# Delta-rule attention and a top-1 mixture of experts: weight splits moved between steps, slot counts kept in PSUM, the last result block in halves

## The chip, the cores and the metric

The kernel runs on one core of a Trainium2 chip. The metric is the device time of one execution in microseconds, as a median of several runs.

## What is computed

The reference has two stages. The first is an attention with a delta rule: each of 4 x 8 heads carries a state of 48 x 48 that each token reads and then updates. The second sends each of the 3,072 rows of x (384 wide) to the one of eight experts that has its largest logit.

```python
for t in range(S):                       # S = 768, D = 48
    kt, vt, bt = (k_n[:, :, t], v[:, :, t], beta[:, :, t, None])
    y[:, :, t] = np.einsum('bhd,bhde->bhe', q[:, :, t], state)
    v_old = np.einsum('bhde,bhd->bhe', state, kt)
    state = state + bt[:, :, :, None] * np.einsum('bhd,bhe->bhde', kt, vt - v_old)
...
logits = x @ w_gate                      # x: 3072 x 384, 8 experts
expert_idx = np.argmax(logits, axis=1)
...
for e in range(E):
    h = np.maximum(x[expert_idx == e] @ w1[e], 0.0)      # 384 -> 1024
    out[expert_idx == e] = gate_w[expert_idx == e, None] * (h @ w2[e])
```

## The kernel before

**Steps.** The 3,072 tokens are 24 blocks of 128, n = 0 to 23, four batch entries by six stretches of time. A block needs the state that the block four before it left. Each is solved in four sub-blocks of 32 rows, and the sub-blocks of four different blocks run in one step, so that the steps t = 0 to 26 form a skewed pipeline: block n begins in step n and ends in step n + 3. Lines 967 to 1016 issue a step, in this order: mask, residual(t) (TensorE L446 and L458, then VectorE's L465, which subtracts it from v), the x rows of the block that has just ended (TensorE L543 into a bank `xp`, ScalarE L544 copying the row out), apply(t) (TensorE L473, four copies of ScalarE L478 to `u`), and finish(t-3) in four parts: L493, the small products L279 with ScalarE's copy L291 (`pm`), the state products L503 into a bank `sb` with ScalarE's copies L507 (`st`, which the residual of the next step reads), and L513 with L517 (`yt`, which the next x rows read).

**Places.** Between these parts stand seven calls beside(t, 0) to beside(t, 6), the places 0 to 6 of a step. There the other work is issued: loads that are due (list `off`), the inverses of the blocks to come (VectorE), the slot groups (up to FINE[i] parts of a generator a place), weight splits where the table WSL names (t, i), and pieces of expert 0's early work where ES does. The order in which an engine takes instructions is the order of issue, so these tables set each queue by hand.

**Slots.** When a group of blocks has ended (four blocks up to n = 11, two up to 19, one from 20 on; W4 = 12, W1 = 4), emit_slots (L547) finds each row's expert and its place in the expert's list. VectorE makes the one-hot matrix `ohb` in five operations (L562 to L579). TensorE counts into columns of the bank `xp` that hold no x rows: `ohb` by a triangle of ones (L584) and by ones (L587), each group anew. VectorE adds a running `base` (L593), moves it on (L594), masks the positions (L607) and reduces them to slots (L620). POOL then scatters the rows by indirect DMA (L628) to a table in DRAM. The row buffers come from pool `rp`, tag "row", with two buffers (L524 to L526). After block 17 (EU = 18) expert 0's first two blocks of tokens can be read: load_main(0, 0, 2) at L636. The last two blocks (DEF = 2) do not go through DRAM; for them VectorE makes a selection matrix `one` (L616), and TensorE multiplies the rows by it (L848).

**Weight splits.** Products of expert weights run on pairs of high and low parts. split (L665) is a ScalarE cast (L666) and a VectorE subtraction (L667) from a raw buffer; SP then loads the next raw piece into a ring of three. Eight of these stand in the loop, by WSL.

**The tail.** Expert 0 is started early on its first two blocks of tokens, in the order of the string EO: x (transposes L806), h (a block of the first layer), y (a result block, 24 matmuls L792), and t and o, which are parts of rest() (L835): the third block's transposes, then the last 64 columns, from the late rows (L848) and from a part read from DRAM (L850). The places of these in the loop are ES, and after the loop EF. dummy(8) and dummy(3) in rest() are filler matmuls without a use of their own (L660). After the tail the pool `lp` is closed and the experts 0 to 7 run one after the other; L782 is their first layer.

Of the kernel before, what the change touches and what calls it, by code (L numbers as in the profile page):

```python
# [8 lines left out]
F32 = mybir.dt.float32  # L9
# [33 lines left out]
def deltanet_moe(ctx, tc, qT, kT, kr, v, beta, w_gate, w1, w2, out):  # L43
# [27 lines left out]
    def constants():  # L71
        nc.gpsimd.memset(esel, 0.0)
        for p in range(NP):
# [8 lines left out]
        nc.gpsimd.memset(ones, 1.0)  # L82
        iota(last_i, [[1, CAP - 128 * NG]], 128 * NG)
# [28 lines left out]
    W1 = 4  # L112
# [6 lines left out]
    EU = 18  # L119
    TS = 5  # L120
# [15 lines left out]
    sb_ = [pss.tile([128, 512], F32, name=f"sb{j}")[:, 0:2 * NP * D].rearrange("p (b n d) -> p b n d", b=2, n=NP)  # L136
           for j in range(2)]
# [344 lines left out]
    def finish(n):  # L482
# [16 lines left out]
        if not last:  # L499
            sb = sb_[b // 2][:, b % 2]  # L500
            for h in range(H):
                r = slice(64 * (h % 2), 64 * (h % 2) + D)
                nc.tensor.matmul(sb[r, h // 2, :], lhsT=tiles[tb][b]["kn"][:, h], rhs=u[:, h, :],  # L503
                                 start=(tb == 0 and b % 2 == 0 and h < 2), stop=True, skip_group_check=True)
# [41 lines left out]

    def emit_slots(tb, b, w, parts, rl):  # L547
# [3 lines left out]
        def small(nm, shape, dt=F32):  # L551
            return lp.tile(shape, dt, name=f"{nm}{tb}_{b}", tag=f"{nm}{w}", bufs=1 if w > 1 else 2)
# [36 lines left out]
        dst = xg if tb * B + b < NN - DEF else xt  # L589
# [3 lines left out]
        V.tensor_tensor(out=pos, in0=both(base), in1=pp[:, 0:w, :], op=ALU.add)  # L593
        V.tensor_tensor(out=base, in0=base, in1=pp[:, w, :], op=ALU.add)  # L594
# [5 lines left out]
        if tb * B + b + w == NN - DEF:  # L600

            V.scalar_tensor_tensor(out=base, in0=lim, scalar=float(128 * NG - CAP), in1=base, op0=ALU.add, op1=ALU.max)
            nc.scalar.copy(out=late, in_=base)
        if tb * B + b + w == EU:
            V.scalar_tensor_tensor(out=base, in0=lim, scalar=float(128 * G0 - CAP), in1=base, op0=ALU.add, op1=ALU.max)

        noted(V.tensor_tensor(out=pos, in0=pos, in1=ohb, op=ALU.mult))  # L607
# [27 lines left out]
        if tb * B + b + w == EU:  # L635
            load_main(0, 0, G0)  # L636
        if tb * B + b + w == NN - DEF:
# [160 lines left out]
    def early():  # L798
# [36 lines left out]
    def rest():  # L835
# [450 lines left out]
```

## Time and profile before

| | us |
|---|---|
| median of 3 runs | 525.61 (523.99 to 525.97) |
| the profiled execution | 521.81 |
| its span | 519.70 |
| TensorE busy in the span | 482.6 (93%) |
| VectorE | 339.5 (65%) |
| ScalarE | 254.1 (49%) |
| POOL | 112.3 (22%) |

Times in the text are microseconds from the start of the span of the profiled execution, and names such as L473 are lines of the kernel before. A bracket behind a row of the timeline gives the time that the engine stood idle ahead of it and what ended that. A row gathers instructions of one kind that follow one another: x64 are 64 of them, and the time beside it is that of all.

### The profile page before, as it was taken

How to read it: one execution, taken by the hardware profiler on the slowest of the kernel's cores; microseconds unless marked ns; L12 is line 12 of the kernel's file. 1: busy time of each engine (PE TensorE's matmuls, PEld its weight loads, DVE VectorE, ACT ScalarE, POOL GpSimd, SP SyncE). 2: the span in 40 equal slices, each digit the busy share in tenths (PEclk: the TensorE clock that was granted, in tenths of full speed). 3: DMA queues.
4: the chain of work that ended last, by engine and by line, in shares of the span. 5: the costliest groups of instructions: out<-in, count | busy, mean ns of one | idle time of the engine just before them, and what ended most of it. 6: DMA issues, size and time to landing. Idle time of an engine off the chain costs nothing.

```text
span 519.7 us, 17366 instructions
## 1 busy us (share of the span) xinstructions
PE 482.6 (93%) x7298; PEld 432.6 (83%) x7298; DVE 339.5 (65%) x982; ACT 254.1 (49%) x537; POOL 112.3 (22%) x146
## 2 busy tenths in 40 slices
PE   7799998998998979988999999999999999999991
PEld 5656787887887868777888999999999999999991
DVE  2999969799799996545332976465656656565310
ACT  3512557585856735865442564544446444444210
POOL 6010121242331522322221002103030210303111
PEclk8699999999999969989999999999999999999997
DMA  6588748848565333544042596374847547481000
GB/s 206 126 211 266 182 137 189 223 117 218 160 156 152 90 131 126 177 158 132 18 118 67 159 224 169 126 176 121 182 136 169 158 136 159 142 192 38 13 19 26
DMA packets 74844, 74.14 MB, mean 143 GB/s; under 512 B 46649, under 2 KB 62506, under 8 KB 74764
## 3 DMA queue, kind: packets, MB, share of 16 engines
q1 hardware_dynamic: 71308, 63.45, 47.1%
q0 software_dynamic: 3456, 9.57, 5.0%
q8 instruction: 58, 0.95, 0.8%
q14 instruction: 22, 0.18, 0.1%
HBM read 54.25 MB, written 19.42 MB: 142 GB/s over the span
## 4 chain that ended last, share of the span: by engine, by line
PE 73%; DVE 15%; ACT 4%; issue 3%; DMA 2%; POOL 1%; SPq 0%; ACTq 0%; DVEq 0%; POOLq 0%
PE h L782 23%; PE y L792 19%; PE y L1092 4%; DVE lw L380 4%; PE pq L279 4%; PE pg L279 3%; PE xp L543 3%; PE ks L446 3%; PE ks L473 3%; PE yp L513 2%; PE wm L660 2%; DVE ta L369 2%; PE yp L493 2%; DMA kt<-in_kT_dram 2%; PE ks L458 2%
## 5 line engine op out<-in xcount | busy, mean ns | idle before, releaser
L792 PE MATMUL y<-w2h,hx 128*128 128x384 f32 x352 | 93.2, 339 | 0.0
L795 POOL DMA_INDIRECT out_dram<-yo,idx x32 | 40.3, 1259 | 203.0 <-ACT yo L1087 115.8
L792 PEld LDWEIGHTS y<-w2h,hx 128*128 128x128 f32 x352 | 64.0, 188 | 0.7 <-DVE hx L786 0.6
L782 PE MATMUL h<-xh,w1l 128*128 128x448 f32 x168 | 61.3, 365 | 0.0
L782 PE MATMUL h<-xh,w1h 128*128 128x448 f32 x168 | 61.3, 365 | 0.0
L782 PE MATMUL h<-xl,w1h 128*128 128x448 f32 x168 | 61.1, 363 | 0.0
L478 ACT COPY u<-ks 32x384 f32<-32x384 f32 x96 | 45.1, 469 | 32.2 <-PE ks L473 25.2
L667 DVE TENSOR_TENSOR w2l<-w2r,w2h 128x768 fp32r<-128x768 f32 x32 | 31.4, 983 | 44.9 <-ACT w2h L666 44.3
L792 PE MATMUL y<-w2l,hx 128*128 128x384 f32 x176 | 59.4, 337 | 0.0
L786 DVE SCALAR_TENSOR_TENSOR hx<-h,hx 128x448 fp32r<-128x448 f32 (+1 forms) x64 | 37.4, 586 | 29.0 <-ACT hx L785 28.3
L785 ACT ACTIVATE hx<-h 128x448 fp32r<-128x448 f32 (+1 forms) x64 | 33.2, 518 | 46.5 <-PE h L782 46.5
L298 POOL TENSOR_SCALAR_AFFINE_SELECT pm<-pm 128x1024 f32<-128x1024 f32 x24 | 26.2, 1091 | 111.2 <-DVE tb L369 31.7
L1087 ACT ACTIVATE yo<-y,gt 128x384 f32<-128x384 f32 x22 | 12.8, 582 | 64.0 <-PE y L792 36.4
L446 PE MATMUL ks<-st,kt 112*32 112x96 f32 x768 | 43.3, 252 | 0.4 <-ACT st L507 0.3
L667 DVE TENSOR_TENSOR w1l<-w1r,w1h 128x1024 fp32r<-128x1024 f32 x24 | 30.0, 1252 | 11.7 <-ACT w1h L666 11.2
L380 DVE TENSOR_TENSOR lw<-lw,ta 128x31 f32<-128x31 f32 (+7 forms) x96 | 36.9, 384 | 0.2
L446 PEld LDWEIGHTS ks<-st,kt 112*32 112x32 f32 x768 | 32.3, 111 | 5.0 <-issue 1.0
L279 PE MATMUL pg<-kt 48*128 48x128 f32 x384 | 31.4, 314 | 4.4 <-DMA kt<-in_kT_dram 3.5
L544 ACT COPY row<-xp 128x384 f32<-128x384 f32 x24 | 11.5, 479 | 46.4 <-PE xp L543 46.4
L279 PEld LDWEIGHTS pg<-kt 48*128 48x128 f32 x384 | 28.1, 219 | 7.3 <-issue 4.3
L782 PEld LDWEIGHTS h<-xh,w1l 128*128 128x128 f32 x168 | 31.5, 188 | 2.6
L782 PEld LDWEIGHTS h<-xl,w1h 128*128 128x128 f32 x168 | 31.5, 188 | 2.4
(162 smaller groups left out, 1026.1 us busy)
## 6 DMA issues: line engine op xcount, KB each, us to landing
w1r<-in_w_dram SPq DMA_DIRECT2D x24, 512.0 KB
w2r<-in_w_dram SPq DMA_DIRECT2D x32, 384.0 KB
xg<-zrow SPq DMA_DIRECT2D x14, 394.0 KB
kt<-in_kT_dram SPq DMA_DIRECT2D x24, 224.0 KB
qt<-in_qT_dram SPq DMA_DIRECT2D x24, 224.0 KB
xr<-xg SPq DMA_DIRECT2D x28, 168.0 KB
ku<-in_kr_dram SPq DMA_DIRECT2D x20, 192.0 KB
v_all<-in_v_dram SPq DMA_DIRECT2D x15, 192.0 KB
```

Source lines behind the costliest of these rows:

```text
L279: ins = nc.tensor.matmul(pg[a][:, p], lhsT=kt[r, p], rhs=xt[r, p], start=True, stop=True, tile_position=(64 * a, 0), skip_group_check=True)
L298: ins = nc.gpsimd.affine_select(out=pm, in_=pm, compare_op=ALU.is_gt, fill=0.0, base=0, pattern=[[0, H], [1, C]], channel_multiplier=-1)
L380: tiles["mark"] = noted(nc.vector.tensor_tensor(out=y, in0=y, in1=x, op=ALU.subtract))
L446: nc.tensor.matmul(ks[32 * q:32 * q + 32, 2 * p:2 * p + 2, :], lhsT=kt_t[n % KTL][0:RP, p, 32 * q:32 * q + 32], rhs=st_view(n % B, p), sta ...
L478: nc.scalar.copy(out=uview(n)[r], in_=ks[r])
L667: nc.vector.tensor_tensor(out=lo, in0=src, in1=hi.bitcast(F32), op=ALU.subtract)
L782: nc.tensor.matmul(ps, lhsT=w[:, d, fs], rhs=x_[:, d], start=(n == 0), stop=(n == len(terms) - 1))
L785: nc.scalar.activation(out=hh, in_=ps, func=AF.Relu)
L786: nc.vector.scalar_tensor_tensor(out=hl, in0=ps, scalar=0.0, in1=hh.bitcast(F32), op0=ALU.max, op1=ALU.subtract)
L792: nc.tensor.matmul(ps, lhsT=h(f)[h_], rhs=w2[w][:, f, :], start=(n == 0), stop=(n == len(terms) - 1))
L795: nc.gpsimd.indirect_dma_start(out=out, out_offset=bass.IndirectOffsetOnAxis(ap=idx, axis=0), in_=yo, in_offset=None, bounds_check=N - 1, ...
L1092: nc.tensor.matmul(ps[0:2 * w], lhsT=h2[:, f], rhs=w_[:, f, :], start=(n == 0), stop=(n == len(terms) - 1))
```

## The change

1. The splits at place 6 of steps 21 to 23 move to place 1 (table WSL).
2. Blocks 16 to 19 are slot groups of their own (W1 from 4 to 8), and so each has its own row buffer and its own VectorE operations.
3. The counts are summed in PSUM over all groups. They lie in columns 384 on of the bank that holds the first of the two state tiles (`sbt[0]`). begin(n) writes the base there, at n = 0, 18 and 22, as a product with a matrix of 1/128; behind() adds to a group's columns what the group before it left, by `utri` (ones without the triangle). The positions are then one VectorE operation, the bank times `ohb`.
4. The load of expert 0's first tokens goes to place 4 of step 22 (XRL).
5. In the tail the second result block of expert 0 is cut into two halves of 12 matmuls (second(..., half)), and the parts of rest() stand between them: the third block's transposes (t), the DRAM part and the first late row (p), the other late row and the split (o). The fillers are gone. The small tiles and the output tile of that block lie in pool `rp`.
6. POOL makes two more constants at the start.

```diff
-    W1 = 4
+    W1 = 8
+    XRL = (22, 4)
-    WSL = ((20, 1), (20, 3), (21, 3), (21, 6), (22, 3), (22, 6), (23, 3), (23, 6))
+    WSL = ((20, 1), (20, 3), (21, 1), (21, 3), (22, 1), (22, 3), (23, 1), (23, 3))
-    EF = (4, 6, 8, 9, 10, 12, 13, 14, 15)
-    EO = 'xxxhhhhhhhhytyo'
+    EF = (4, 5)
+    EO = 'xxxhhhhhhhhytypoy'
...
+    def running(n):
+        i = (n >= EU) + (n >= NN - DEF)
+        k, at = ((4, 384), (2, 424), (1, 448))[i]
+        return sbt[0][:, at:at + (k + 1) * E].rearrange("p (j e) -> p j e", e=E), k
+    def count(out, lhsT, rhs, start=False):
+        nc.tensor.matmul(out, lhsT=lhsT, rhs=rhs, start=start, stop=True, skip_group_check=True)
+    def begin(n):
+        pp, k = running(n)
+        count(pp, part_, base.unsqueeze(1).broadcast_to([128, k + 1, E]), n == 0)
+    def behind(pp, k, w):
+        if "ohb" not in tiles:
+            return
+        w0, oh0 = tiles["ohb"]
+        count(pp[:, k - w:k], utri, oh0[:, w0 - w:w0])
+        for i in range(w0 - w + 1, w0):
+            count(pp[:, k - w:k - w0 + i], ones, oh0[:, i:i + 1].broadcast_to([128, w - w0 + i, E]))
...
-        pp = tiles["bank"][:, NP * (2 * D + E):NP * (2 * D + E) + (w + 1) * E].rearrange("p (j e) -> p j e", e=E)
-        nc.tensor.matmul(pp[:, 0:w, :], lhsT=ltri, rhs=ohb, start=True, stop=False, skip_group_check=True)
-        for j in range(1, w + 1):
-            for i in range(j):
-                nc.tensor.matmul(pp[:, j, :], lhsT=ones, rhs=ohb[:, i], start=False, stop=(i == j - 1),
-                                 skip_group_check=True)
+        if n0 in (EU, NN - DEF):
+            begin(n0)
+        else:
+            behind(pp, k, w)
+        tiles["ohb"] = (w, ohb)
+        count(pp[:, k - w:k], ltri, ohb)
+        for i in range(w):
+            count(pp[:, k - w + i + 1:k + 1], ones, ohb[:, i:i + 1].broadcast_to([128, w - i, E]))
...
-        V.tensor_tensor(out=pos, in0=both(base), in1=pp[:, 0:w, :], op=ALU.add)
-        V.tensor_tensor(out=base, in0=base, in1=pp[:, w, :], op=ALU.add)
+        noted(V.tensor_tensor(out=pos, in0=pp[:, k - w:k], in1=ohb, op=ALU.mult))
...
-        noted(V.tensor_tensor(out=pos, in0=pos, in1=ohb, op=ALU.mult))
...
-        if tb * B + b + w == EU:
-            load_main(0, 0, G0)
+        if n1 == EU:
+            off.append((XRL, lambda: load_main(0, 0, G0)))
+            off.sort(key=lambda x: x[0])
...
-        dummy(8)
         pt = psg_[-1].tile([128, KD, w], F32, name="xt4", tag="g")
         for d in range(KD):
-            for i, (row, one) in enumerate(last):
-                nc.tensor.matmul(pt[:, d], lhsT=dims(row[:, 0:DM], d), rhs=one, start=(d + i == 0), stop=False, skip_group_check=True)
-        for d in range(KD):
-            nc.tensor.matmul(pt[:, d], lhsT=dims(xr[0:w, NG, 0:DM], d), rhs=ident[0:w, 0:w], start=False, stop=True,
+            nc.tensor.matmul(pt[:, d], lhsT=dims(xr[0:w, NG, 0:DM], d), rhs=ident[0:w, 0:w], start=(d == 0), stop=False,
                              skip_group_check=True)
+        for i in range(DEF):
+            if i == DEF - 1:
+                yield
+            row, one = last[i]
+            for d in range(KD):
+                nc.tensor.matmul(pt[:, d], lhsT=dims(row[:, 0:DM], d), rhs=one, start=False, stop=(i == DEF - 1),
+                                 skip_group_check=True)
         split(x[0][:, :, 128:], x[1][:, :, 128:], pt)
-        dummy(3)
```

How the order moves is seen at three places. The lines are those of each kernel: L549, L483, L296, L512 and L522 of the changed one are L544, L478, L291, L507 and L517 of the one before, L470 is L465, and L697 and L698 are the split's L666 and L667. In these rows the numbers behind a name are a tile's own: row4_1 is the row buffer of block 17 (stretch 4, batch entry 1), row4_0 before that of the pair 16 and 17, row4_2 that of block 18; a bracket names the queues and engines that the instruction waits for.

ScalarE in step t=21, before:

```order
L544 COPY row4_0_4316<-xp4_1_4467 128x384 [waits PE_49]
L478 COPY u18_3781<-ks21_4425 32x384 [waits DVE_49,PE_49]
L478 COPY u21_4326<-ks21_4425 32x384 [waits Activation_49,Pool_49]
L291 COPY pm1_110<-pq4_3_0_4533 128x4x128 [waits PE_49,Activation_49]
L666 CAST w1h0_4395<-w1r0_1_4328 128x1024 [waits DMAHW0_49]
L507 COPY st2_128<-sb1_98 48x4x48 [waits PE_49]
L599 COPY row4_0_4316<-ids2_81 128x2x2
L517 COPY yt4_2_4577<-yp4_2_0_4522 128x2x128 [waits PE_49,Activation_49]
L666 CAST w1h0_4395<-w1r0_2_4399 128x1024 [waits DMAHW2_49]
L544 COPY row4_2_4628<-xp4_2_4629 128x384 [waits DMASW7_49,DMASW6_49,PE_49]
```

ScalarE in the same step after the change:

```order
L549 COPY row4_1_4475<-xp4_1_4476 128x384 [waits DMASW6_49,DMASW7_49,PE_49,Activation_49]
L697 CAST w1h0_4395<-w1r0_1_4324 128x1024 [waits DMAHW0_49]
L483 COPY u18_3770<-ks21_4432 32x384 [waits DVE_49,PE_49]
L483 COPY u21_4322<-ks21_4432 32x384 [waits Pool_49]
L296 COPY pm1_112<-pq4_3_0_4546 128x4x128 [waits PE_49]
L697 CAST w1h0_4395<-w1r0_2_4399 128x1024 [waits DMAHW2_49]
L512 COPY st2_130<-sb1_98 48x4x48 [waits PE_49]
L630 COPY row4_1_4475<-ids2_81 128x2
L522 COPY yt4_2_4592<-yp4_2_0_4535 128x2x128 [waits PE_49,Activation_49]
L549 COPY row4_2_4639<-xp4_2_4640 128x384 [waits DMASW0_49,PE_49,Activation_49]
```

The copy of block 17's row now waits for two queues of POOL's scatters (DMASW), the first split of the step stands ahead of the copies to u, and the split that stood at the step's end stands ahead of the state copies.

VectorE from the group of block 17 to the subtraction of step t=22, before:

```order
L579 TENSOR_TENSOR ohb4_0_4481<-oh4_0_4477,m24_0_4479 128x16 [waits DVE_49]
L667 TENSOR_TENSOR w1l0_4396<-w1r0_1_4328,w1h0_4395 128x1024 [waits DMAHW0_49,Activation_49]
L593 TENSOR_TENSOR pos4_0_4549<-base_77,xp4_1_4467 128x16 [waits PE_49]
L594 TENSOR_TENSOR base_77<-base_77,xp4_1_4467 128x8 [waits DVE_49]
L605 SCALAR_TENSOR_TENSOR base_77<-lim_78,base_77 128x8 [waits DVE_49]
L607 TENSOR_TENSOR pos4_0_4549<-pos4_0_4549,ohb4_0_4481 128x16
L667 TENSOR_TENSOR w1l0_4396<-w1r0_2_4399,w1h0_4395 128x1024 [waits DMAHW2_49,Activation_49]
L465 TENSOR_TENSOR v_all_105<-v_all_105,ks22_4585 128x384 [waits PE_49]
```

VectorE there after the change:

```order
L606 TENSOR_TENSOR ohb4_1_4490<-oh4_1_4486,m24_1_4488 128x8 [waits DVE_49]
L698 TENSOR_TENSOR w1l0_4396<-w1r0_1_4324,w1h0_4395 128x1024 [waits DMAHW0_49,Activation_49]
L698 TENSOR_TENSOR w1l0_4396<-w1r0_2_4399,w1h0_4395 128x1024 [waits DMAHW2_49,Activation_49]
L625 TENSOR_TENSOR pos4_1_4561<-sb0_97,ohb4_1_4490 128x8 [waits DVE_49,PE_49]
L632 SCALAR_TENSOR_TENSOR base_77<-lim_78,sb0_97 128x8
L650 TENSOR_REDUCE sli4_1_4579<-pos4_1_4561 128x1 [waits DVE_49]
L470 TENSOR_TENSOR v_all_107<-v_all_107,ks22_4596 128x384 [waits PE_49]
```

Of the small operations one on the position and one on the base are left. The split that stood last, next to the subtraction from v, now stands ahead of the small operations, behind the split moved to place 1.

TensorE in the tail, before (of rows that repeat, one stands):

```order
L792 MATMUL y0_1_5404<-w2h0_4707,he7_5248 128x384
L584 MATMUL xp5_3_5388<-ohb5_3_5402,ltri_74 128x8 [waits Activation_49]
L587 MATMUL xp5_3_5388<-ohb5_3_5402,ones_75 128x8
L660 MATMUL wm6_5450<-zrow_82 128x512 [waits PE_49]
L848 MATMUL xt4_5459<-one2_5361,row5_2_5277 128x64
L848 MATMUL xt4_5459<-one3_5444,row5_3_5387 128x64 [waits DVE_49]
L850 MATMUL xt4_5459<-ident_68,xr0_4682 128x64 [waits DMAHW7_49]
L660 MATMUL wm7_5471<-zrow_82 128x512 [waits PE_49]
L782 MATMUL h0_0_5501<-xb0_5367,w1h0_4395 128x192 [waits PE_49,Activation_49]
```

TensorE in the tail after the change:

```order
L824 MATMUL y0_1_5420<-w2h0_4658,xe_4902 128x384
L559 MATMUL sb0_97<-ohb5_2_5309,utri_99 128x8 [waits DVE_49]
L559 MATMUL sb0_97<-ohb5_3_5418,ltri_74 128x8 [waits DVE_49]
L559 MATMUL sb0_97<-ohb5_3_5418,ones_75 128x8
L882 MATMUL xt4_5438<-ident_68,xr0_4741 128x64 [waits DMAHW7_49,PE_49]
L889 MATMUL xt4_5438<-one2_5377,row5_2_5294 128x64 x3
L889 MATMUL xt4_5438<-one3_5450,row5_3_5403 128x64 [waits DVE_49,Activation_49]
L824 MATMUL y0_1_5420<-w2h0_4658,he4_5153 128x384
L824 MATMUL y0_1_5420<-w2h0_4658,he7_5265 128x384
L813 MATMUL h0_0_5504<-xb0_5383,w1h0_4395 128x192 [waits Activation_49]
```

The fillers are gone, the DRAM part (L882) stands ahead of the late rows (L889), and half of the result block stands behind them.

## Rows read from the trace of the kernel before

**Rows 1.** Windows: us, busy of PE, PEld, DVE, ACT, POOL; PEclk, DMA share, GB/s.

```profile
282.90:505.10 222.20, 222.19 (x1210) 214.05 (x1211) 128.39 (x218) 100.53 (x170) 36.37 (x28) 1.00 0.53 137
209.40:237.70 28.30, 23.55 (x650) 20.08 (x648) 14.91 (x36) 20.59 (x46) 6.64 (x9) 0.94 0.54 169
```

**Rows 2.** Timeline, PE, t=21 to 24: start, us, line, operation [idle before <-releaser].

```profile
214.09 1.16 PE L279 MATMUL pq<-qt,kt 48*128 48x128 f32 x16
...
216.74 0.86 PE L446 MATMUL ks<-st,kt 112*32 112x96 f32 x24
...
222.14 0.88 PE L473 MATMUL ks<-v_all,wt 32*32 32x48 f32 x64 [1.87 <-DVE v_all L465]
...
223.55 2.08 PE L279 MATMUL pq<-qt,kt 48*128 48x128 f32 x16
...
227.55 0.86 PE L446 MATMUL ks<-st,kt 112*32 112x96 f32 x24
...
230.96 0.88 PE L473 MATMUL ks<-v_all,wt 32*32 32x48 f32 x64 [0.62 <-DVE v_all L465]
...
237.27 0.49 PE L806 MATMUL xt<-ident,xr 128*128 128x128 f32 x2 [0.97 <-DVE xe L667]
...
237.69 0.86 PE L446 MATMUL ks<-st,kt 112*32 112x96 f32 x24
```

**Rows 3.** Timeline, PE, steps t=16 to 19.

```profile
168.78 1.11 PE L543 MATMUL xp<-esel,yt 128*128 128x104 f32 x8 [0.31 <-DVE pos L607]
...
173.69 0.86 PE L446 MATMUL ks<-st,kt 112*32 112x96 f32 x24
...
181.19 0.86 PE L446 MATMUL ks<-st,kt 112*32 112x96 f32 x24
...
186.07 0.29 PE L458 MATMUL ks<-u,gg 128*32 128x48 f32 x1 [3.15 <-issue]
...
186.28 2.04 PE L543 MATMUL xp<-esel,yt 128*128 128x104 f32 x8
...
195.27 1.29 PE L446 MATMUL ks<-st,kt 112*32 112x96 f32 x24
```

**Rows 4.** Timeline, DVE, end of step t=21.

```profile
219.87 1.75 DVE L667 TENSOR_TENSOR w1l<-w1r,w1h 128x1024 fp32r<-128x1024 f32 x1 [0.58 <-ACT w1h L666]
```

**Rows 5.** Chain that ended last, from 272.85 to 282.9: start us, us, what.

```profile
272.85 4.20 PE y L792 x24
...
277.09 1.75 PE wm L660 x8
278.84 1.98 PE xt L848 x12
280.81 1.19 PE xt L850 x6
282.01 0.77 PE wm L660 x3
```

**Rows 6.** Timeline, ACT, step t=21.

```profile
212.79 0.48 ACT L544 COPY row<-xp 128x384 f32<-128x384 f32 x1 [1.33 <-PE xp L543]
...
213.63 1.94 ACT L478 COPY u<-ks 32x384 f32<-32x384 f32 x4 [0.36 <-PE ks L473]
...
215.48 1.05 ACT L291 COPY pm<-pq 128x512 f32<-128x512 f32 x2
...
216.43 1.04 ACT L666 CAST w1h<-w1r 128x1024 fp32r<-128x1024 f32 x1
...
217.38 0.63 ACT L507 COPY st<-sb 48x192 f32<-48x192 f32 x2
```

**Rows 7.** Timeline, POOL, second scatter of blocks 14 and 15.

```profile
208.45 0.97 POOL L628 DMA_INDIRECT xg<-row,sli  x1 [0.30 <-issue]
```

**Rows 8.** DMA issues, 208.4 to 208.6: queue, kind, count, median us to landing.

```profile
xg<-row,sli POOLq DMA_INDIRECT x1, 5.8
```

**Rows 9.** Timeline, DVE, last slot group.

```profile
277.80 0.25 DVE L616 TENSOR_SCALAR one<-last_i,sl 128x64 f32<-128x64 f32 x1
```

More of the change, by code (lines that the diff above doesn't have):

```diff
@@ L82, in constants @@
         nc.gpsimd.memset(ones, 1.0)
+        nc.gpsimd.memset(part_, 1.0 / 128)
+        nc.gpsimd.tensor_tensor(out=utri, in0=ones, in1=ltri, op=ALU.subtract)
         iota(last_i, [[1, CAP - 128 * NG]], 128 * NG)
@@ L135, in deltanet_moe @@
     pg_ = lp_.enter_context(ExitStack())
-    sb_ = [pss.tile([128, 512], F32, name=f"sb{j}")[:, 0:2 * NP * D].rearrange("p (b n d) -> p b n d", b=2, n=NP)
-           for j in range(2)]
+    sbt = [pss.tile([128, 512], F32, name=f"sb{j}") for j in range(2)]
+    sb_ = [t[:, 0:2 * NP * D].rearrange("p (b n d) -> p b n d", b=2, n=NP) for t in sbt]
+    utri = lp.tile([128, 128], BF16, name="utri")
+    part_ = lp.tile([128, 128], F32, name="part_")
     psg_ = [pg_.enter_context(tc.tile_pool(name="psg", bufs=GB, space=PSUM))]
@@ L503, in finish @@
                 nc.tensor.matmul(sb[r, h // 2, :], lhsT=tiles[tb][b]["kn"][:, h], rhs=u[:, h, :],
-                                 start=(tb == 0 and b % 2 == 0 and h < 2), stop=True, skip_group_check=True)
+                                 start=(tb == 0 and b == 2 and h < 2), stop=True, skip_group_check=True)
             for a in range(2):
@@ L551, in small @@
         def small(nm, shape, dt=F32):
-            return lp.tile(shape, dt, name=f"{nm}{tb}_{b}", tag=f"{nm}{w}", bufs=1 if w > 1 else 2)
+            return lp.tile(shape, dt, name=f"{nm}{tb}_{b}", tag=f"{nm}{w}", bufs=1 if w > 1 and nm != "ohb" else 2)
         def wide(t):
@@ L582, in emit_slots @@
             yield
[L583 to L589 removed]
+        n0 = tb * B + b
+        n1 = n0 + w
+        pp, k = running(n0)
+        if n0 in (EU, NN - DEF):
[6 more added lines that the diff above has]
+            count(pp[:, k - w + i + 1:k + 1], ones, ohb[:, i:i + 1].broadcast_to([128, w - i, E]))
+        dst = xg if n0 < NN - DEF else xt
         pos = small("pos", [128, w, E])
@@ L786, in relu, with second @@
         nc.vector.scalar_tensor_tensor(out=hl, in0=ps, scalar=0.0, in1=hh.bitcast(F32), op0=ALU.max, op1=ALU.subtract)
-    def second(ps, h, w2):
+    def second(ps, h, w2, half=0):
         terms = [(h_, w, f) for f in range(KF) for h_, w in ((0, 0), (0, 1), (1, 0))]
         for n, (h_, w, f) in enumerate(terms):
-            nc.tensor.matmul(ps, lhsT=h(f)[h_], rhs=w2[w][:, f, :], start=(n == 0), stop=(n == len(terms) - 1))
+            if half == 0 or half == 1 + (f >= KF // 2):
+                nc.tensor.matmul(ps, lhsT=h(f)[h_], rhs=w2[w][:, f, :], start=(n == 0), stop=(n == len(terms) - 1))
     def scatter(yo, idx):
@@ L825, in early @@
                 yield
-        gt, idx = smalls(0, 0, G0, lp)
+        gt, idx = smalls(0, 0, G0, rp)
         for g in range(G0):
             ps = psg_[-1].tile([128, DM], F32, name=f"y0_{g}", tag="g")
-            second(ps, lambda f: [h[:, g * 128:g * 128 + 128] for h in hs[f]], WW[0]["w2"])
-            yo = lp.tile([128, DM], F32, name=f"yo0_{g}", tag="u", bufs=UB)
+            for half in (1, 2) if g == G0 - 1 else (0,):
+                if half == 2:
+                    yield
+                second(ps, lambda f: [h[:, g * 128:g * 128 + 128] for h in hs[f]], WW[0]["w2"], half)
+            yo = (lp.tile([128, DM], F32, name=f"yo0_{g}", tag="u", bufs=UB) if g < G0 - 1 else
+                  rp.tile([128, DM], F32, name=f"yo0_{g}", tag="row", bufs=2))
             nc.scalar.activation(out=yo, in_=ps, func=AF.Copy, scale=gt[:, g:g + 1])
@@ L916, in deltanet_moe @@
     ks_ = ks_[2 * B:]
+    begin(0)
     dummy(W0)
@@ L947, in ahead_step @@
         if order and not (order[0] == "o" and len(last) < DEF):
-            run(other if order.pop(0) in "to" else ahead)
+            run(other if order.pop(0) in "tpo" else ahead)
     def beside(t, i):
```

13 lines of the change are left out of this document (8 added, 5 removed).

## The prediction

> **What bounds the kernel now.** I read the table of windows first. From 282.9 to 505.1 TensorE is busy for 222.19 of 222.20 us [rows 1]: experts 0 to 7 run there back to back, and nothing that ends earlier on another engine can shorten that. So the question is what moves the start of expert 0's first layer at 282.9. In the steps from 209.4 to 237.7 TensorE is busy for 23.55 of 28.30 us, at a mean granted clock of 0.94 [rows 1]: here are waits, and a dip of the clock.
>
> The timeline of TensorE in those steps is next [rows 2]. A step begins with the 24 matmuls of L446, at 216.74, 227.55 and 237.69: the steps of t=22 and t=23 take 10.8 and 10.1 us, where the one of t=17 takes 181.19 − 173.69 = 7.5 [rows 3]. At t=22 the products of L473 begin after 1.87 us without work, which VectorE's L465 ended; then the 16 matmuls of L279 take 2.08 us against 1.16 at t=21. That is TensorE at 1.2 GHz in place of 2.4. From L279 to the next step's first matmul it is 227.55 − 223.55 = 4.00 us against 216.74 − 214.09 = 2.65, so the dip costs 1.35 us. VectorE's timeline tells what L465 stood behind [rows 4]: the subtraction of a weight split, 1.75 us from 219.87, which place 6 of the step before put there. At t=23 the same happens in small, 0.62 us of idle TensorE ahead of L473, and at the end of that step a third such subtraction delays the transposes of L806 by 0.97 us [rows 2].
>
> Last I read the chain of waits from 272.85 on [rows 5]: 24 matmuls of expert 0's second result block (4.20 us), the counts, 8 fillers of L660 (1.75), the late rows (1.98), the rest of that tile (1.19), 3 fillers (0.77), and 0.13 us of gap to the first layer at 282.91.
>
> **The change, part by part.** The sum is made against the profiled execution, 521.81 us with a span of 519.70, which is 3.80 under the median of the runs shown (525.61).
>
> *Fewer small operations per slot group.* Three VectorE operations become one. In the step of t=16 L543 waits 0.31 us for the last of the three [rows 3]; it no longer reads the bank that they share, so 0.3 goes. In one more group VectorE has no idle time ahead of them and I take 0.2; in the others it waits longer for other things. In sum −0.5 (0 to −1.0, three such waits). TensorE's count matmuls, 8 or 16 columns wide, change by a few per group: a group of four loses two, a pair gains one, a single gains one, there are two more groups, and three products with fp32 bases come in. No row shows the fp32 form; L473, fp32 with 48 columns, takes 0.88 us for 64 [rows 2], so the cost is near nothing; I take +0.1 (0 to +0.3).
>
> The counts now lie in a bank of the state products L503, from which ScalarE copies the state, two copies in 0.63 us [rows 6]. In five groups VectorE's read of the positions gets a wait for ScalarE. The bounds are 0 and +0.6 for each group where nothing covers the copy; I take 0, because in all five a longer VectorE operation stands ahead of the position. The Trainium skill, PSUM — Partial Sum Buffer, section "PSUM bank collisions raise a hardware error", speaks against this part: two engines must not touch one bank and quadrant at once, reads included, so copy and position take turns. By that rule alone the cost would be up to 5 × 0.63 = 3.1 us, an estimate; no run here shows a collision.
>
> *Splits and single blocks, t=21 to 24.* I work this through ScalarE's timeline [rows 6]. Before, the row copy of block 17 begins at 212.79; then come u (1.94), pm (1.05), a split (1.04) and st (0.63). After, block 17 has a row buffer of its own, and its copy waits for the two scatters of blocks 14 and 15, whose buffer it takes. The later one is issued at 208.45 and needs 5.8 us to land [rows 7, 8]: 214.25. So the copy runs from 214.3, 1.5 us later. Behind it on ScalarE stand the split moved to place 1 (ends at 215.8), u (217.7), pm (218.6), the second split (219.6) and st (220.2, was 218.0). The residual of t=22 needs st: it ends near 221.1, L465 follows at once since no split precedes it, and L473 begins at 222.2, where it was 222.14 [rows 2]. The row's wait takes the place of the split's: 0 us.
>
> From there two things are won: no split stands ahead of L465 of t=23 or the last transposes of that step, and the 1.35 us of the dip, if TensorE keeps 2.4 GHz. Against it ScalarE has, in each of these steps, 0.48 + 2 × 1.04 + 1.94 + 1.05 + 0.63 = 6.2 us of work in a row [rows 6] before st is done, and that sets the step. I get L473 of t=23 at 229.6 (was 230.96) and the start of t=24 at 236.7 (was 237.69): **−1.0 us**. Bounds: −3.0, if the copy need not wait and ScalarE's gaps close; +1.5, if the wait stays and the steps win nothing.
>
> Expert 0's first load of tokens moves from the end of block 17's slots to place 4 of t=22, past SP's weight loads. Its readers, the transposes of L806, come a step later (the last at 237.27 [rows 2]); I take 0.
>
> *The tail.* The fillers go, 1.75 + 0.77, with the gap of 0.13 [rows 5]; one more count matmul comes in, some 0.05 (the counts lie between 277.05 and 277.09). What they hid was VectorE's `one` of the last block, done at 277.80 + 0.25 = 278.05 [rows 9], 0.96 us after the counts. Now the identity products (1.19) and half of the late rows (0.99) are issued ahead of it, 2.2 us. The split of the tile's last columns, which ran in the 0.9 us from 282.01 to 282.91, lies beside the second half of the result block, 4.20/2 = 2.1 us. So 1.75 + 0.77 + 0.13 − 0.05 = 2.6; I take **−2.5** (−2.7 to −1.5, which is 1 us missing of either cover).
>
> Sum: −0.5 + 0.1 − 1.0 − 2.5 = **−3.9 us**; the bounds add up to −6.7 and +0.3. Against the median 525.61 that is **521.7 us** (517.9 for a profiled execution). The ends do not come together; the case's own range is 519.5 to 523.5.
>
> **The rivals.**
> *The row copy need not wait.* If the scatters land 1.5 us sooner, t=21 wins that as well: −5.4, 520.2 us. For it: the weight loads beside them are issued at other places now. Against it: the scatter's own place is the same, and 5.8 us is what it took [rows 7, 8].
>
> *The stall of t=18 goes.* There TensorE stands for 3.15 us and the profile names no releaser [rows 3]; then it works at 1.2 GHz (L543 2.04 us against 1.11 [rows 3]), and the step takes 195.27 − 181.19 = 14.1 us where the one before takes 7.5. The program is laid out anew, so this may not recur: −3.9 − 6.6 = −10.5, 515.1 us. For it: no engine of the program is named as its cause. Against it: that step's work is the same, and with the cause unknown it may stay.
>
> *The clock falls at t=22 all the same.* TensorE will idle there for about 2 us again, now ahead of the residual (st is 2.2 us later) in place of L473; 1.87 us of idle time came before the fall, 0.62 and 0.97 brought none [rows 2]. Then the 1.35 us stay: −2.5, 523.1 us. The Trainium skill, TensorE: Matmul & The Clock Gate, section "Part 1: The HAM clock gate", has the throttled clock as the default, which recent activity releases. By that rule an idle time ahead of the residual counts like one ahead of L473; the trace's one fall here agrees.
>
> *ScalarE becomes the bound, and TensorE slow step after step.* This is the case on the other side. With two splits in each step of t=21 to 23, each of the next steps may open with TensorE idle for 1.5 to 2 us, and run at 1.2 GHz as a whole. The price of such a step is seen at t=18: from L543 to the next step 195.27 − 186.28 = 9.0 us, against 173.69 − 168.78 = 4.9 at t=16 [rows 3], so 4.1. One brings −3.9 + 4.1 = +0.2, no change; from two on it is slower: +4.3, 529.9 us. For it: 6.2 us of ScalarE in a row with the row's wait in front. Against it: t=23 has two splits already, and there TensorE waits for only 0.62 and 0.97 us.
>
> *The tail wins little.* The change does not do what it says, if `one`, the late row or the other half is not ready in time and the wait takes 2 of the 2.5 us: −1.9, 523.7 us. For it: the covers are 2.1 and 2.2 us and no row shows them. Against it: 0.96 and 0.9 us are all they have to cover.
>
> **How the numbers follow.** Some 0.5%, 2.6 us, is what a measurement can tell from no change, so faster is below 523.0. Forecast 0.38 (0.32 of it below 523.0), row copy without wait 0.12, stall gone 0.10, clock falls 0.18 (0.07 below), tail 0.10 (all same), ScalarE's series 0.12 (0.10 slower, 0.02 same). Faster 0.32 + 0.12 + 0.10 + 0.07 = 0.61; same 0.06 + 0.11 + 0.10 + 0.02 = 0.29; slower 0.10. The range leaves out the stall's case and the series, near 2 in 10: low 517.0 (the bound −6.7 gives 518.9, less the 2 us over which the runs of before are spread), high 527.0 (+0.3 gives 525.9, and one slow step 525.8, with 1 us of spread).
>
> **What would show it.** After the change: the row copy of block 17 idle until the scatter has landed, near 214.3; no split ahead of L465's successor in t=22 and t=23; L279 of t=22 at 1.16 us, not 2.08; the step of t=24 some 1.0 us sooner after the one of t=21; no L660 between the last x rows and the first h, and that distance 2.5 us shorter. I am wrong if the stretch from t=21 to t=24 is as long as before, if the tail has a wait of over 1 us, or if a stall of several us without releaser stands elsewhere, or nowhere.

## The result, and the profile after

Over 18 runs each the changed kernel takes 520.85 us (515.86 to 526.58), the kernel before 525.68 (521.38 to 531.06). The ratio is 0.9914, with a 95% interval of 0.9889 to 0.9939: 4.5 us faster (3.2 to 5.8), where 3.9 was forecast. The ratio leaves out the few executions over 1.5% above the fastest of their kernel, so it is not quite that of the two medians.

The two profiles don't show this if only their spans are set side by side: 519.7 us before and 520.7 after. The profiled execution of the changed kernel took 522.53 us, over its median, and that of the kernel before 521.81, under it. One execution of this program differs from the next by several us, so the pieces have to be read. The starts of the steps give these:

| us | before | after | after, second profile |
|---|---|---|---|
| start of the span to the first step (t=0) | 34.8 | 36.2 | 34.2 |
| first step to step t=21 | 174.5 | 175.6 | 171.9 |
| t=21 to t=24 | 28.3 | 27.5 | 28.3 |
| t=24 to t=26 | 23.9 | 25.1 | 24.6 |
| t=26 to expert 0's first layer | 21.3 | 19.1 | 19.1 |
| first layer to the end of the span | 236.8 | 237.2 | 237.3 |

These are TensorE's rows of the changed kernel in the steps t=21 to t=24, in the timeline (L451, L478, L284, L518 and L838 are L446, L473, L279, L513 and L806 of the kernel before):

```profile
215.39 0.88 PE L478 MATMUL ks<-v_all,wt 32*32 32x48 f32 x64
...
220.32 0.86 PE L451 MATMUL ks<-st,kt 112*32 112x96 f32 x24
...
222.01 0.27 PE L451 MATMUL ks<-st,kt 112*32 112x96 f32 x1 [0.49 <-ACT st L512]
...
223.85 0.90 PE L478 MATMUL ks<-v_all,wt 32*32 32x48 f32 x64
...
225.28 1.16 PE L284 MATMUL pq<-qt,kt 48*128 48x128 f32 x16
...
232.75 0.37 PE L478 MATMUL ks<-v_all,wt 32*32 32x48 f32 x14 [0.67 <-issue]
...
235.62 0.69 PE L838 MATMUL xt<-ident,xr 128*128 128x128 f32 x2 [0.65 <-ACT pm L296]
236.34 1.95 PE L518 MATMUL yp<-pm,u 128*48 128x128 f32 x16
...
239.27 1.50 PE L451 MATMUL ks<-st,kt 112*32 112x96 f32 x24
```

The wait of 1.87 us at t=22 is gone, and L284 takes 1.16 us there, not 2.08 [rows 2]: the step takes 7.8 us in place of 10.8. But the step t=21 is longer (8.5 for 7.4), and at the end of t=23 TensorE goes to 1.2 GHz (1.95 and 1.50 us for work that takes 1.05 and 0.86), into t=24; the mean granted clock is 0.82 in t=23 and 0.90 in t=24 (0.91 and 0.95 in the second profile). ScalarE's timeline shows what stands in t=21, against [rows 6]:

```profile
216.13 0.48 ACT L549 COPY row<-xp 128x384 f32<-128x384 f32 x1 [2.24 <-DMA xg<-row,sli]
216.51 1.05 ACT L697 CAST w1h<-w1r 128x1024 fp32r<-128x1024 f32 x1
...
221.33 0.63 ACT L512 COPY st<-sb 48x192 f32<-48x192 f32 x2
```

The row copy waits for the scatter, as foreseen: it begins 4.3 us into the step, where 4.9 was forecast. The chain of waits in the tail, against [rows 5]:

```profile
275.93 2.10 PE y L824 x12
278.03 0.07 PE sb L559 x3
278.11 1.19 PE xt L882 x6
279.30 2.24 PE xt L889 x12
281.54 2.17 PE y L824 x12
```

No filler and no gap is left between these pieces. Behind them the first layer begins, and 12 us on stands a wait that the kernel before did not have. TensorE's timeline shows it, VectorE's a wait for the late rows (`xs`) ahead of it, and SP's queue the load of these rows:

```profile
295.64 0.61 PE L824 MATMUL y<-w2h,hx 128*128 128x384 f32 x2 [0.42 <-DVE hx L817]
```

```profile
289.83 0.17 DVE L1076 TENSOR_TENSOR xr<-xr,xs 128x10 f32<-128x10 f32 x1 [0.32 <-DMA xs<-xt]
```

```profile
283.82 4.00 SPq L737 DMA_DIRECT2D xs<-xt  x7
```

VectorE adds the late rows ahead of some of the activations `hx` in its queue. Their load now waits for TensorE's second half of the result block, and it is issued 0.3 us after the first layer starts; before, 0.7 us ahead of it (282.24 against 282.91). So part of the tail's gain, some 0.4 us here, is given back.

### The profile page after: what moved, and what is told of

Read it like the earlier page. It is cut to its first block, busy times and chain, and to the rows that moved or that the text cites. A ratio compares the mean times of both kernels' runs of the same rounds, so it can differ in the third digit from the quotient of the medians.

```text
span 520.7 us, 17340 instructions
## 1 busy us (share of the span) xinstructions
PE 484.5 (93%) x7286; PEld 434.8 (83%) x7291; DVE 337.7 (65%) x975; ACT 254.7 (49%) x539; POOL 112.8 (22%) x148
## 4 chain that ended last, share of the span: by engine, by line
PE 50%; issue 1%; ACT 1%; DMA 1%; SPq 1%; DVE 1%; POOL 1%; ACTq 0%; POOLq 0%
PE h L813 21%; PE y L824 18%; PE y L1131 4%; PE xp L548 1%; PE yp L518 1%; DMA w1r<-in_w_dram 1%; SPq L737 1%; PE ks L451 1%; PE ks L478 1%; PE pq L284 1%; PE ks L463 1%; PE xt L889 0%; POOL out_dram L827 0%; PE yp L498 0%; ACT pm L296 0%
## 5 line engine op out<-in xcount | busy, mean ns | idle before, releaser
L483 ACT COPY u<-ks 32x384 f32<-32x384 f32 x96 | 45.1, 469 | 33.7 <-PE ks L478 23.6
L698 DVE TENSOR_TENSOR w2l<-w2r,w2h 128x768 fp32r<-128x768 f32 x32 | 30.6, 957 | 40.6 <-ACT w2h L697 40.0
L451 PE MATMUL ks<-st,kt 112*32 112x96 f32 x768 | 43.5, 253 | 0.7 <-ACT st L512 0.5
L451 PEld LDWEIGHTS ks<-st,kt 112*32 112x32 f32 x768 | 32.4, 111 | 5.5 <-issue 1.9
L284 PE MATMUL pg<-kt 48*128 48x128 f32 x384 | 31.7, 317 | 5.2 <-DMA kt<-in_kT_dram 4.2
L698 DVE TENSOR_TENSOR w1l<-w1r,w1h 128x1024 fp32r<-128x1024 f32 x24 | 29.4, 1225 | 9.0 <-ACT w1h L697 8.6
L478 PE MATMUL ks<-v_all,wt 32*32 32x48 f32 x1536 | 25.8, 206 | 10.1 <-DVE v_all L470 6.6
L284 PEld LDWEIGHTS pg<-kt 48*128 48x128 f32 x384 | 28.3, 222 | 8.3 <-issue 5.2
L658 POOL DMA_INDIRECT xg<-row,sli x22 | 22.6, 1028 | 58.0 <-ACT yt L522 20.4
L478 PEld LDWEIGHTS ks<-v_all,wt 32*32 32x32 f32 x1536 | 21.4, 107 | 16.4 <-DVE v_all L470 9.8
```

The lines of the kernel that those rows point to most:

```text
L284: ins = nc.tensor.matmul(pg[a][:, p], lhsT=kt[r, p], rhs=xt[r, p], start=True, stop=True, tile_position=(64 * a, 0), skip_group_check=True)
L451: nc.tensor.matmul(ks[32 * q:32 * q + 32, 2 * p:2 * p + 2, :], lhsT=kt_t[n % KTL][0:RP, p, 32 * q:32 * q + 32], rhs=st_view(n % B, p), sta ...
L478: ins = nc.tensor.matmul(ks[r, h, :], lhsT=tiles[n // B]["wt"][r, n % B * H + h, :], rhs=vn[r, h, :], start=True, stop=True, tile_position ...
L483: nc.scalar.copy(out=uview(n)[r], in_=ks[r])
L698: nc.vector.tensor_tensor(out=lo, in0=src, in1=hi.bitcast(F32), op=ALU.subtract)
```

## The experiments

Each but the second profile of the kernel before ran 6 or 12 times beside the kernel before, and each has one profile. Four of them (the tail alone, the counts alone, splits and pairs as before, and pairs with the first tokens later) ran on another chip, where the kernel before took 528.2 us and not 525 to 526. Their ratios are against that, and the changed kernel was not timed there, so beside its ratio they have to be read with care. The theory at first: the gain is the tail (2.2 to 2.5 us), the steps t=21 to t=24 (1 us) and the counts (0.5). The rival: the new program only moves the waits that the profile names no releaser for, and the dips of the clock.

**The changed kernel again.** No edit.

> The changed kernel once more, for a second profile beside the first and for the others of this call to be set against. Both theories: about 4.5 us below the kernel before (ratio near 0.991). In the profile: by the first theory (the gain is made in the tail and in the steps t=21 to 24, by the sum of the parts) the distance from the start of step t=26 to expert 0's first layer is again 19.2 us, where it was 21.3 before, and the steps from t=21 to t=26 take less than 52.2 us unless the clock falls. By the rival (the new program only moves the waits that the profile names no releaser for, and dips of the clock) those waits stand at other places than in the first profile of the same kernel, and the stretch ahead of t=21 differs by several us from one profile to the next.

Ratio 0.9895 (0.9858 to 0.9932); the table has its pieces. The first theory's 19.1 us in the tail are there; t=21 to t=26 take 52.9 us, with a fall of the clock in t=23. The rival is right on the stretch ahead of t=21: 175.6 and 171.9 us for one and the same kernel. In all the profiles of this study that stretch takes 171.9 to 175.6 us. So its sum tells nothing of the change; single steps in it are read below.

**The tail put back.**

```diff
-    EF = (4, 5)
-    EO = 'xxxhhhhhhhhytypoy'
+    EF = (4, 6, 8, 9, 10, 12, 13, 14, 15)
+    EO = 'xxxhhhhhhhhytyo'
...
+        dummy(8)
...
+        dummy(3)
```

> The changed kernel with its tail put back: whole result block, 8 and 3 fillers, late rows ahead of the DRAM part. First theory: 2.2 to 2.5 us slower than the changed kernel, so about 2.0 us below the kernel before (ratio near 0.996), and 21.3 us from the start of step t=26 to the first layer. Rival (the gain lies in the loop or in where waits fall): as fast as the changed kernel, ratio near 0.991.

Ratio 0.9966 (0.9932 to 1.0001): with the old tail most of the gain is gone, 2.7 us against the changed kernel's first ratio and 3.7 against its second. The profile has 22.3 us from t=26 to the first layer, and 239.3 us from there, 2.0 to 2.1 more than the changed kernel. The table of windows shows the reason, for the 6 us ahead of the first layer and the 6 behind it (columns as in [rows 1]):

```profile
277.93:283.93 6.00, 5.85 (x28) 4.04 (x26) 0.60 (x3) 0.44 (x3) 1.93 (x2) 0.85 0.18 68
283.93:289.93 6.00, 6.00 (x32) 6.00 (x33) 1.85 (x3) 1.93 (x5) 0.00 (x0) 0.58 0.42 104
```

The granted clock falls at the last three fillers (1.46 us, where [rows 5] has 0.77) and stays low into the first layer. That does not make the fillers its cause. In four of the ten profiles of the new tail, which has none, the clock falls too, at or just behind the late rows' products, and TensorE shows no idle time in the 6 us ahead of the first layer. This is such a window, of the run with fewer inverses below:

```profile
276.45:282.45 6.00, 6.00 (x28) 5.93 (x27) 0.36 (x1) 0.32 (x1) 0.97 (x1) 0.72 0.10 36
```

In both tails the 18 products for `xt`, 64 columns wide, stand ahead of the fall. Whether they start it was not tried. No run takes out the fillers alone, so what they and the halves are worth apart was not tried.

**The tail alone, in the kernel before.** The new functions `second` and `rest`, EO, EF and the places of the small tiles, all as in the change, and nothing else:

```diff
-    EO = 'xxxhhhhhhhhytyo'
+    EO = 'xxxhhhhhhhhytypoy'
...
-        dummy(8)
...
-        dummy(3)
```

> The kernel before with the new tail alone (halves, late rows by parts, no fillers). First theory (the tail makes most of the gain, by its fillers and by the dips of the clock that followed them in two of three profiles of the old tail): 19.1 us from step t=26 to the first layer in place of 21.3, the rest of the program up to 0.4 us longer, and 2 to 3.5 us below the kernel before, ratio 0.993 to 0.996. Rival (the tail's gain is given back by waits in the experts, or needs the other parts): less than 1 us, ratio above 0.998.

Ratio 0.9897 (0.9841 to 0.9953), 5.4 us (2.5 to 8.4), where 2 to 3.5 was expected; 18.9 us from t=26 to the first layer, then 237.3 with a wait of 0.64 us for `hx`. The tail alone brings a gain as large as that of the whole change, within these intervals.

**The splits at their old places.** 

```diff
-    WSL = ((20, 1), (20, 3), (21, 1), (21, 3), (22, 1), (22, 3), (23, 1), (23, 3))
+    WSL = ((20, 1), (20, 3), (21, 3), (21, 6), (22, 3), (22, 6), (23, 3), (23, 6))
```

> The changed kernel with the three splits back at place 6 of steps 21 to 23. First theory: the 1.87 us idle time of TensorE ahead of the products of step t=22 comes back, with the dip of the clock: 1 to 2 us slower than the changed kernel, ratio near 0.994. Rival (the row's wait has taken the place of the split's, and nothing is won in these steps): no slower than the changed kernel, ratio 0.991 or less.

Ratio 0.9897 (0.984 to 0.9954), which can't be told from the changed kernel. In the profile the waits come back (TensorE stands 1.64 us ahead of L478 at t=22 and 1.16 at t=23), and t=21 to t=26 take 55.9 us in place of 52.6 and 52.9. At t=22 L284 still takes 1.16 us; the clock falls at t=23, where it takes 2.08. So the first theory has the wait, and the time (five executions, an interval of 3 us either way) can neither show nor exclude what it costs.

**Pairs for blocks 16 to 19.**

```diff
-    W1 = 8
+    W1 = 4
```

> The changed kernel with blocks 16 to 19 as two pairs again; splits, counts and tail as changed. First theory (single blocks cost the row's wait and win nothing in the chain): the step t=21 takes 7.4 us, the time is 0.5 to 2 us below the changed kernel's. Rival (single blocks spread the scatters, and pairs delay the first load of expert 0's tokens or the last slot operations): the time is 0.5 to 2 us above the changed kernel's, with a wait for the tokens of L806's successor at t=23.

Ratio 0.9879 (0.9835 to 0.9924). The steps t=21 and t=22 take 7.4 and 7.6 us, but t=23 takes 12.3. The timeline of TensorE:

```profile
233.70 0.66 PE L838 MATMUL xt<-ident,xr 128*128 128x128 f32 x2 [2.22 <-DMA xr<-xg]
```

The last scatter of blocks 16 and 17 is issued 7.2 us into t=22 and not 3.4, and the load of expert 0's tokens 12.1 us after that step's start and not 7.6. So single blocks buy the tokens in time and pay for it at t=21: t=21 to t=24 take 27.3 us with pairs, 27.5 and 28.3 without. Both theories hold half.

**Splits and pairs as before.** The two edits above together.

> The changed kernel with both the splits and the pairs of blocks 16 to 19 as before; counts and tail as changed. Steps t=21 to t=26 take 51.2 us with new splits and pairs, 52.6 to 52.9 with new splits and single blocks, 56.0 with old splits and single blocks. First theory (the two parts are tied: single blocks alone cost some 3 us there, the new splits win 1 to 3 us, and together they change little): 52 to 53 us in these steps as in the kernel before, with the 1.87 us wait at t=22, and the time 0.5 to 1.5 us above that of the changed kernel with pairs. Rival (single blocks cost nothing, the 56.0 were an accident of one execution): 55 to 56 us here too.

52.3 us from t=21 to t=26, and a wait of 1.68 us at t=22, as the first theory had it; the ratio is 0.9864 (0.9793 to 0.9934). With neither of the two parts the kernel can't be told from that with both.

**Row buffers without the wait.** Blocks 16 and 17 share one buffer.

```diff
-            t = pool.tile([128, 2 if n < NN - 2 else 1, ROW], F32, name=f"row{tb}_{b}", tag=tag, bufs=2)
+            if w == 1 and n < NN - 2 and n % 2:
+                t = tiles["row1"][:, 1:2]
+            else:
+                t = tiles["row1"] = pool.tile([128, 2 if n < NN - 2 else 1, ROW], F32, name=f"row{tb}_{b}", tag=tag, bufs=2)
```

> The changed kernel, with blocks 16 and 17 in the two halves of one row buffer (18 and 19, 20 and 21 likewise), so that the copy of block 17's row has no scatter to wait for. In the profiles of the changed kernel so far that copy stands idle for 2.2 and 3.4 us until the scatter of blocks 14 and 15 has landed. First theory (this wait gives back at t=21 and t=22 what the moved splits win): ScalarE idles for about 1.7 us ahead of the copy, as in the step before, the step t=21 takes 7.4 us and not 8.5 or 9.5, and the time is 1 to 2 us below the changed kernel's. Rival (ScalarE's queue sets these steps anyway, or the wait moves to the next row): same time, and the step t=22 longer by what t=21 wins.

Ratio 0.9901 (0.9865 to 0.9937). ScalarE's wait for the scatter is gone, as these rows of its timeline and TensorE's show (it idles for the x rows, as before the change), but the step t=21 takes 8.5 us all the same (210.01 to 218.56):

```profile
213.79 0.48 ACT L552 COPY row<-xp 128x384 f32<-128x384 f32 x1 [1.60 <-PE xp L551]
```

```profile
217.37 0.39 PE L508 MATMUL sb<-u,ku 128*48 128x48 f32 x8 [0.63 <-issue]
```

The scatter's wait was real, and not what sets the step. The changed kernel has the same 0.64 us of idle time inside L508 in this step, and the kernel with pairs has none; the row names no releaser, so what single blocks cost there is left open. From t=21 to t=26 it is 51.7 us here, within what the same loop gives from one profile to the next (51.6 to 52.9).

**Counts as before.** The old counting in the changed kernel:

```diff
-        noted(V.tensor_tensor(out=pos, in0=pp[:, k - w:k], in1=ohb, op=ALU.mult))
+        V.tensor_tensor(out=pos, in0=both(base), in1=pp[:, 0:w, :], op=ALU.add)
+        V.tensor_tensor(out=base, in0=base, in1=pp[:, w, :], op=ALU.add)
...
+        noted(V.tensor_tensor(out=pos, in0=pos, in1=ohb, op=ALU.mult))
...
-    begin(0)
```

> The changed kernel with the counts as before: each group counted anew in the bank of the x rows, three VectorE operations on it. First theory: 0.3 to 0.5 us slower than the changed kernel, which can't be told from none in the time; in the profile the x rows wait 0.3 us for the positions at t=16 again. Rival (the counts in PSUM cost waits for ScalarE, or the early product at the start delays the first step, which began 1.4 us later in the changed kernel's profile): 0.5 to 1.5 us faster than the changed kernel, and the first step begins near 34.8 us again.

Ratio 0.9937 (0.9899 to 0.9974): 1.2 us slower than the changed kernel by its first ratio and 2.2 by its second, where 0.3 to 0.5 was expected, with intervals that overlap. The x rows at t=16 wait 0.32 us again. The first step began at 34.9 us; with the early product it begins at 34.2 to 36.2 in ten profiles, without it at 34.7 to 35.1 in four, so no delay by it is shown.

**The counts alone, in the kernel before.** The same lines the other way, with running, begin, behind and the two constants.

> The kernel before with the counts kept in PSUM and nothing else. First theory (x rows no longer wait for VectorE's positions, above all at t=18, where VectorE is the bound): 0.5 to 2 us below the kernel before, ratio 0.996 to 0.999; at t=18 the x rows run at once and the wait stands ahead of the products of L473's successor. Rival (VectorE sets the end of t=18 either way, since the inverses are as long): same time, ratio 0.999 to 1.001.

Ratio 0.9954 (0.9917 to 0.9991), 2.4 us faster by its middle: more than the 0.4 forecast. The place is t=18. TensorE's timeline there, of the changed kernel's second profile, against [rows 3]:

```profile
180.21 0.86 PE L451 MATMUL ks<-st,kt 112*32 112x96 f32 x24
...
181.86 1.03 PE L548 MATMUL xp<-esel,yt 128*128 128x104 f32 x7
...
186.41 0.88 PE L478 MATMUL ks<-v_all,wt 32*32 32x48 f32 x64 [3.00 <-DVE v_all L470]
187.82 1.92 PE L284 MATMUL pq<-qt,kt 48*128 48x128 f32 x16
...
191.85 0.86 PE L451 MATMUL ks<-st,kt 112*32 112x96 f32 x24
```

And VectorE's, of the kernel before:

```profile
185.14 0.16 DVE L594 TENSOR_TENSOR base<-base,xp 128x8 f32<-128x8 f32 x1
...
187.08 0.55 DVE L465 TENSOR_TENSOR v_all<-v_all,ks 128x384 f32<-128x384 f32 x1
```

Before, the x rows (L543) could not run until L593 and L594 had read the counts in their bank. In this profile they began only at 186.28, and at 1.2 GHz they still ran when the subtraction L465 was done at 187.63; L473 began at 188.25, 7.1 us into the step. After, they run at once, and L478 begins when L470 is done, 6.2 us into the step.

But this profile is the exception. In the other three with the old counts the x rows are over first, and L473 follows the subtraction within 0.1 us, 6.5 us into the step. TensorE in the second profile of the kernel before:

```profile
187.26 1.11 PE L543 MATMUL xp<-esel,yt 128*128 128x104 f32 x8 [0.52 <-DVE base L594]
189.49 1.50 PE L473 MATMUL ks<-v_all,wt 32*32 32x48 f32 x64 [1.12 <-DVE v_all L465]
```

What sets L473 there is VectorE, which has hardly an idle moment between the end of one subtraction and the start of the next. The table of windows has this stretch, ahead of t=18's subtraction, for the kernel before, the changed kernel (second profile) and the run with fewer inverses below (the third pair of numbers is VectorE's busy time and its operations):

```profile
176.66:187.08 10.42, 7.11 (x216) 6.00 (x216) 10.21 (x47) 4.63 (x12) 3.23 (x4) 0.95 0.51 148
175.72:185.81 10.09, 7.42 (x226) 6.29 (x224) 9.92 (x45) 5.16 (x13) 3.01 (x4) 1.00 0.55 156
179.28:189.59 10.31, 7.20 (x225) 6.21 (x223) 10.14 (x45) 5.16 (x13) 3.12 (x4) 1.00 0.42 129
```

The two operations fewer bring the subtraction on some 0.3 us sooner. In four profiles with the old counts the step t=18 takes 13.1 to 14.1 us (mean 13.5); in ten with the new ones 10.8 to 13.2 (mean 12.2). Of these 1.3 us, 0.6 lie ahead of L473, and 0.7 behind it, where the clock stays at 2.4 GHz through these products in four of the ten (0.88 us, as above) and in none of the four (1.46 to 1.50). Why it stays up longer is not shown.

**Fewer inverses ahead of the subtraction.**

```diff
-    STEPS = (3, 3, 3, 3, 2, 2, 2)
+    STEPS = (2, 2, 3, 3, 3, 3, 2)
```

> The changed kernel with STEPS (2, 2, 3, 3, 3, 3, 2) in place of (3, 3, 3, 3, 2, 2, 2): as many parts of the inverses in a step, but two fewer ahead of the subtraction from v. It tests what the step t=18 is bound by: it takes 11 to 14 us in every profile so far, with TensorE idle for 2.4 to 3.2 us. First theory (VectorE's inverses stand ahead of the subtraction there, so that the stall is no accident of the program's layout): the idle time ahead of the products of t=18 is shorter by 0.5 to 1 us, those at t=9 to 16 are shorter too, and the time is 1 to 3 us below the changed kernel's. Rival (VectorE is bound by the sum of its work up to the last inverse, wherever it stands): same time, the wait comes at the end of the inverses instead. Second rival (the stall has nothing to do with VectorE): no change at t=18.

Ratio 0.993 (0.989 to 0.9969), no faster; t=18 takes 13.2 us, and TensorE stands there longer:

```profile
190.19 1.50 PE L478 MATMUL ks<-v_all,wt 32*32 32x48 f32 x64 [3.72 <-DVE v_all L470]
```

This does not test what it was meant to. A step issues its subtraction ahead of all its seven places, and STEPS adds up to 18 either way, so as many parts as before stand between two subtractions: VectorE runs 45 operations ahead of that of t=18 in both kernels, 36 of them of the inverses, as the windows above show for the sum. So the theory on their order stays untested. The rival, that VectorE is bound by the sum of its work there, agrees with its idle time of 0.2 us in 10.

**The kernel before again.** No edit, one execution.

> The kernel before once more, for a second profile. First theory: the step t=18 takes about 14 us again with the x rows held until VectorE has read the counts of the pair 12 and 13; the steps t=21 to t=26 take 52 us again, 21.3 us lie from step t=26 to the first layer. Rival (these were accidents of one execution): the step t=18 takes 7 to 8 us, or the long wait stands in another step.

It took 524.75 us. The step t=18 takes 13.1 us, t=22 has its 1.87 us wait, t=21 to t=26 take 53.1 us. From t=26 to the first layer it is 21.3, then 238.4 us, 1.6 more than in the first profile: the clock falls there, as with the tail put back.

```profile
284.18:290.18 6.00, 6.00 (x39) 6.00 (x40) 2.21 (x4) 2.70 (x5) 0.00 (x0) 0.72 0.38 78
```

**Pairs, and the first tokens later.** With W1 = 4:

```diff
-    ES = ((23, 4), (23, 5), (23, 6), (24, 1), (24, 2),
+    ES = ((23, 6), (23, 6), (23, 6), (24, 1), (24, 2),
```

> A version meant to be faster than both: the changed kernel with pairs for blocks 16 to 19, and the three transposes of expert 0's first tokens all at place 6 of step t=23 (they stood at places 4, 5 and 6), since with pairs TensorE waited there for 2.2 us until the tokens had landed. First theory: that wait is gone or below 0.5 us, the step t=23 takes 10 to 11 us in place of 12.3, and the time is 1 to 2 us below that of the changed kernel with pairs, ratio 0.984 to 0.987. Rival (the tokens come at the same time and the wait moves to the step's end, or the later splits of the tokens delay t=24): same ratio as with pairs, 0.988.

Ratio 0.9846 (0.9784 to 0.9908). The wait for the tokens is still 1.66 us, and t=23 takes 12.0 us, as the rival has it. That the ratio lies in the first theory's range is luck, since its mechanism is not there. Its interval reaches into the changed kernel's, so it is not shown to be better.

## Why the prediction was right, point by point

*The tail: −2.5 forecast, about −3.2 between the means of the profiles.* Where the clock stays at 2.4 GHz, t=26 to the end of the span takes 258.2 us with the old tail (one profile) and 256.0 to 256.5 with the new one (six): −1.7 to −2.1, made of −2.2 to −2.5 up to the first layer and +0.1 to +0.5 behind it. The term was right, and the late load, which the prediction did not price, takes some of it back. What I did not have is the clock. In three of four profiles of the old tail it falls round the first layer, and the stretch takes 259.7, 260.0 and 261.6 us. With the new tail it falls in four of ten, ahead of the first layer, and the stretch takes 257.4 to 257.5. The means are 259.9 and 256.7. By time the tail is worth 2.7 to 3.7 us (put back) or 5.4 (alone, 2.5 to 8.4).

*Steps t=21 to t=24: −1.0 forecast, −0.8 and 0 in two profiles, then given back.* The wait was read rightly: with the old places of the splits TensorE stands 1.6 to 1.9 us ahead of t=22's products in all six profiles, with the new ones in none of eight. The step that failed is "two things are won, … if TensorE keeps 2.4 GHz". The dip's 1.35 us were won at t=22, but t=21 became longer by 1.1 and 2.1 us (8.5 to 9.8 us in seven profiles with single blocks, 7.3 to 8.7 in seven with pairs), and the clock fell one step later, at t=23: t=24 to t=26 take 25.1 and 24.6 us, not 23.9. From t=21 to t=26 it is 52.6 and 52.9 us after and 52.2 and 53.1 before: nothing. A sign of being wrong that the prediction named, a stretch from t=21 to t=24 as long as before, is there in the second profile (28.3 us both). The rival on the clock foresaw a fall, but not this one: ahead of the residual of t=22 TensorE idled 0.49 us, not about 2, and no fall followed there. By the runs, the moved splits and the single blocks together are worth nothing that can be told in the time.

*The counts: −0.4 forecast; −2.4 timed for them alone (−0.5 to −4.4), −1.3 between the means at t=18.* The mis-sized step is "In one more group VectorE has no idle time … and I take 0.2". At t=18 VectorE's two operations fewer give 0.3, near that; the x rows that stood behind the counts, which I left out, cost 0.6 more in one of four profiles; and 0.7 is a clock that falls later. The bound of −1.0 was too near. Ahead of t=21 the profiles scatter by 3.7 us, so the difference between 1.3 and 2.4 stays open. The cost for keeping ScalarE's copies and VectorE's positions apart, taken as 0, did not show: VectorE stands idle ahead of 3 of the 13 positions in the changed kernel's profile, for TensorE each time.

*The other rivals.* The stall of t=18 did not go: it is in all 14 profiles, with steps of 10.8 to 14.1 us. I had taken it for a wait without a cause, as its row says; the cause is VectorE's work between two subtractions, and the release named in that row is no guide. The series of slow steps did not come. The tail was not empty.

So the total, −4.5, came out near the −3.9 forecast by other terms, and that is in part luck: −1.0 did not come, and the tail and the counts gave more than −2.5 − 0.4. The measured parts do not add up closely enough to say how much is whose: −3.2, 0 and −1.3 from the profiles make −4.5, but the two parts timed alone make −5.4 − 2.4 = −7.8, each with an interval of 2 to 3 us either way.

## What to carry to other kernels

When single executions differ by more than the change is worth, compare pieces between fixed points of the program over several profiles, and distrust the piece that varies without a change. When a buffer gets a second reader, ask what the first writer now waits for: here the x rows waited for a count that only lay in the same bank. Then ask whether that wait ends last: in three of four profiles VectorE's work ended after it. Fillers and gaps on the engine that is the bound cost their own length; that they also bring a fall of the clock is not shown.

## What the runs showed that was not expected

The same program has its falls of the clock at other steps from one execution to the next: t=10 takes 9.1 us in one profile of the kernel before, at a mean granted clock of 1.00, and 12.5 at 0.73 in the other, with 0.51 us of idle time in it that no row explains. And the clock falls ahead of the first layer with TensorE busy all the time. What starts them there was not tried.
